# Reading each 4 MB load of keys or values as one contiguous stretch of HBM instead of pieces 256 KB apart

## The chip, the cores and the metric

The kernel runs on one core of a Trainium2 chip. The caches lie in the chip's main memory (HBM). Sixteen DMA engines of the core copy them, packet by packet, into its working memory (SBUF), which has 128 partitions; a kernel asks for such a copy by an instruction on a queue, here that of SP (SyncE). TensorE (PE) multiplies matrices, VectorE (DVE) and ScalarE (ACT) do the rest. The metric is the device time of one execution in microseconds (us). A run of a program on one core is called fast when it lies within 1.5% of the fastest run of the same kernel.

## The reference, cut to what matters

One token attends to a long cache of keys and values. Beside it runs a small gated feed-forward layer, which matters here only because its weights are loaded too.

```python
B, Sq, D = 1, 1, 448
Hq, Hkv, Sk, Dh = 16, 8, 65536, 256           # bf16
k_cache, v_cache: (B, Hkv, Sk, Dh)            # 256 MB (of 2^20 bytes) each
...
scores = einsum("bhqd,bhkd->bhqk", q, k) * Dh ** -0.5
p = softmax(scores, axis=-1)
o = einsum("bhqk,bhkd->bhqd", p, v)
return x + (o reshaped @ wo) + feed_forward(xn)
```

The order in which the 65536 positions of a head are visited is free, so long as keys and values are visited in the same order: the softmax and the weighted sum run over all of them.

## The kernel before: the parts that matter

The ring has four slots of 4 MB (32 KB for each of 128 partitions). Every load fills one slot with 64 rows of 512 B for each partition. The loads go out in one stream from the SP queue, and a load waits only until PE (TensorE) has finished with the slot's former content.

```python
P, CH, NSLOT = 128, 64, 4            # partitions, rows of a partition in a load, slots
FIRST, LAST = [16, 16, 32], [32, 16, 8, 8]     # first and last load are split by rows

def slot_item(key, src, h, n0, parts=None):
    r = rounds[0]; rounds[0] += 1
    s = r % NSLOT
    o = 0
    parts = parts or [("slot%d" % s, CH)]
    for k, (sem, J) in enumerate(parts):
        ap = ring[:, s * SLOT + o * Dh:s * SLOT + (o + J) * Dh]
        item(key + (k,), ap, [(lambda a, J=J: a.rearrange("p (j d) -> p j d", d=Dh),
                               src[0, h].rearrange("(p n) d -> p n d", p=P)[:, n0 + o:n0 + o + J, :])], sem,
             [("FREE", "slot", r - NSLOT)] if r >= NSLOT else None)
        ...

def k_slot(u, c, parts=None):        # half-head u, chunk c; v_slot is the same for values
    slot_item(("k", u, c), A_k_cache, u // 2, (u % 2) * SBN + c * CH, parts)

def prog_sp():                       # the stream of loads
    for key in stream:
        for w in items[key]["need"] or []:
            wait("sp", "pe", w)
        for d, src in items[key]["src"]:
            nc.sync.dma_start(d(items[key]["ap"]), src).then_inc(sems[items[key]["sem"]], 16)
```

With `"(p n) d -> p n d"` and p = 128, partition p owns rows 512p to 512p+511 of a head. A load takes 64 of them: one contiguous piece of 32 KB, and the next partition's piece starts 256 KB further on. PE then transposes the keys (line 382), multiplies them with the query (line 416), and later multiplies the weights of the softmax with the values (line 541).

Of the kernel before, what the change touches and what calls it, by code (L numbers as in the profile page):

```python
# [13 lines left out]
CH = 64  # L14
# [8 lines left out]
def bass_parallel_sum__gqa_block_cached__moe_arch_mod__decode_kernel(  # L23
# [13 lines left out]
    P = 128  # L37
# [223 lines left out]
    def item(key, ap, src, sem, need=None):  # L261
        semtot[sem] = semtot.get(sem, 0) + 16 * len(src)
        items[key] = dict(ap=ap, src=src, sem=sem, val=semtot[sem], need=need)
        stream.append(key)
# [4 lines left out]
    def slot_item(key, src, h, n0, parts=None):  # L269
        r = rounds[0]  # L270
        rounds[0] += 1
# [3 lines that stand above are left out]
        for k, (sem, J) in enumerate(parts):  # L275
            ap = ring[:, s * SLOT + o * Dh:s * SLOT + (o + J) * Dh]
            item(key + (k,), ap, [(lambda a, J=J: a.rearrange("p (j d) -> p j d", d=Dh),
                                   src[0, h].rearrange("(p n) d -> p n d", p=P)[:, n0 + o:n0 + o + J, :])], sem,
                 [("FREE", "slot", r - NSLOT)] if r >= NSLOT else None)
            items[key + (k,)]["rows"] = (n0 + o, J)  # L280
            o += J
        items[key] = dict(parts=len(parts), slot=r)

    def k_slot(u, c, parts=None):
        slot_item(("k", u, c), A_k_cache, u // 2, (u % 2) * SBN + c * CH, parts)

    def v_slot(t, c, parts=None):
        slot_item(("v", t, c), A_v_cache, t // 2, (t % 2) * SBN + c * CH, parts)
# [636 lines left out]
```

## Time and profile before

| | before |
|---|---|
| time | 1291.68 us (1291.57 to 1291.70, 3 runs) |
| bytes loaded | 549 MB (of 10^6 bytes), 22067 packets |
| mean rate | 426 GB/s over the span, 431 GB/s in the middle |
| busy | load queue 99.1% of 16 engines, PE 72%, DVE 43%, ACT 35% |

The page of the kernel before follows: the span, then busy tenths (9 is 90% or more) and GB/s in 40 equal slices, the packets, the queue that carries the loads, and the chain of work that ended last.

```profile
span 1291.1 us, 21412 instructions
...
DMA  9999999999999999999999999999999999999995
GB/s 404 425 433 424 431 432 430 432 429 431 435 428 434 428 434 432 428 435 426 435 433 429 435 427 432 431 432 435 424 436 429 434 431 427 436 429 434 429 431 243
DMA packets 22067, 549.40 MB, mean 426 GB/s; under 512 B 2323, under 2 KB 4374, under 8 KB 4886
...
q1 hardware_dynamic: 22034, 549.04, 99.1%
...
DMA 76%; PE 22%; DVE 1%; ACT 0%; issue 0%; SPq 0%; ACTq 0%
```

The DMA row has no hole before the last slice: loads are queued at all times, or very nearly. The chain contains PE work all the same (22%). A piece of it, in order of time (start, length, what), shows why that is no sign of a PE bound ("issue" is time in which an engine waited for nothing that the profile shows):

```profile
250.73 35.23 DMA ring<-in_A_k_cache_dram
...
293.68 1.90 PE ps_t L382 x16
295.57 0.03 PE ps_s L449 x2
295.60 30.41 DMA ring<-in_A_v_cache_dram
326.01 0.14 issue
326.15 3.29 PE ps_o L541 x32
329.44 0.01 issue
329.46 35.43 DMA ring<-in_A_k_cache_dram
```

Each load in the chain takes 30 to 35 us from its issue to its landing, while 4.19 MB at 431 GB/s need only 9.7 us. So a load stands in a queue of about three loads. The PE pieces of the chain pass while the engines are busy with the loads ahead.

The windows view adds up busy time in stretches. Its columns are the stretch, its length, the busy time of PE, PE's weight loads, DVE, ACT and POOL with instruction counts, the granted clock (the share of TensorE's full clock that its throttle let through), the DMA share and GB/s:

```profile
0.00:30.00 30.00, 15.09 (x216) 13.33 (x216) 15.19 (x33) 9.37 (x16) 4.48 (x34) 1.00 0.96 400
...
300.00:1200.00 900.00, 644.18 (x6678) 465.45 (x6678) 383.34 (x651) 307.80 (x433) 0.00 (x0) 0.85 1.00 431
```

The last two columns say that for 900 us the engines are wholly busy at 431 GB/s.

A busy engine may still be a waiting one: a packet that HBM serves slowly counts as busy (a run further down shows a DMA share of 0.97 at only 383 GB/s). What tells the two apart is how long packets take. The trace has a record of each packet; summed up by size for the kernel before they give (ns):

```
size B   packets  fastest  median    mean   99th pct.
  1792      2048       74      74    76.3       86
  4096       256      159     160   162.3      172
  6272       256      239     239   239.9      251
  8192       404      309     309   312.9      398
 16384       271      611     611   641.7     1099
 32768     16128     1213    1216  1218.1     1227
```

The fastest ones lie on a line. From 4096 to 32768 B it is (1213 - 159) / 28672 = 0.0368 ns for a byte, or 27.2 GB/s for an engine, and 159 - 4096 x 0.0368 = 8.4 ns for a packet. Sixteen engines at 27.2 GB/s make 435 GB/s. The Trainium skill ("DMA: Bandwidth & Descriptors", section "Where 436 GB/s comes from") puts the ceiling of the 16 ports at the same 435 GB/s, and this trace agrees: 431 GB/s in the middle, 1% under it.

### The profile page before, as it was taken

To read this page: it belongs to the slowest core of one execution; us is meant where nothing else is said; L and a number is where in the kernel's file an instruction comes from. 1 tells how busy PE (TensorE), PEld (TensorE's weight loads), DVE (VectorE), ACT (ScalarE), POOL (GpSimd) and SP (SyncE) were. 2 spreads that over 40 slices of the span, in tenths; PEclk is the share of its full clock that TensorE was granted. 3 is DMA by queue.
4 is the path that set the end of the run, shared out by engine and by line. 5 is a ranking of instruction groups with operands and counts; after the bars stand their busy time and mean duration, and the time that the engine had idled before them with its cause. 6 is when DMAs were issued, how large, how long until landed. Compare 5 with 4: busy or idle time off the path is not lost.

```text
span 1291.1 us, 21412 instructions
## 1 busy us (share of the span) xinstructions
PE 934.6 (72%) x9673; PEld 669.9 (52%) x9673; DVE 551.6 (43%) x944; ACT 446.5 (35%) x634; POOL 4.5 (0%) x34
## 2 busy tenths in 40 slices
PE   4988867696666957668587675876669676696665
PEld 4876645464554735546365453654446454474421
DVE  4666435263443625336254352643436353262300
ACT  2556323253332623225233242432424333242300
POOL 1000000000000000000000000000000000000000
PEclk9899879798887988889788897987979888798665
DMA  9999999999999999999999999999999999999995
GB/s 404 425 433 424 431 432 430 432 429 431 435 428 434 428 434 432 428 435 426 435 433 429 435 427 432 431 432 435 424 436 429 434 431 427 436 429 434 429 431 243
DMA packets 22067, 549.40 MB, mean 426 GB/s; under 512 B 2323, under 2 KB 4374, under 8 KB 4886
## 3 DMA queue, kind: packets, MB, share of 16 engines
q1 hardware_dynamic: 22034, 549.04, 99.1%
q8 instruction: 15, 0.25, 0.1%
q14 instruction: 14, 0.11, 0.0%
q10 hardware_dynamic: 4, 0.00, 0.0%
HBM read 549.03 MB, written 0.00 MB: 425 GB/s over the span
## 4 chain that ended last, share of the span: by engine, by line
DMA 76%; PE 22%; DVE 1%; ACT 0%; issue 0%; SPq 0%; ACTq 0%
DMA ring<-in_A_k_cache_dram 42%; DMA ring<-in_A_v_cache_dram 31%; PE ps_t L382 13%; PE ps_o L541 4%; PE ps_q L416 3%; DMA w_area<-in_B_w_down_dram 3%; DMA wr_row<-in_B_w_r_dram 0%; PE ps_s L449 0%; PE ps_t L656 0%; PE ps_m L624 0%; DVE kt_buf L370 0%; ACT S_sb L494 0%; SPq L328 0%; PE ps_m L593 0%; ACT L494 0%
## 5 line engine op out<-in xcount | busy, mean ns | idle before, releaser
L382 PE MATMUL ps_t<-ident_f,ring 128*128 128x128 f32 x4096 | 578.0, 299 | 218.5 <-DMA ring<-in_A_k_cache_dram 217.1
L370 DVE COPY kt_buf<-ps_t 128x1024 bf16<-128x1024 bf16 x768 | 491.9, 685 | 475.8 <-PE ps_t L382 473.6
L382 PEld LDWEIGHTS ps_t<-ident_f,ring 128*128 128x128 f32 x4096 | 502.9, 154 | 343.6 <-DMA ring<-in_A_k_cache_dram 238.5
L372 ACT ACTIVATE kt_buf<-ps_t 128x1024 bf16<-128x1024 bf16 x256 | 261.8, 1023 | 353.3 <-PE ps_t L382 352.9
L394 ACT ACTIVATE s<-ps_q 98x512 bf16<-98x512 f32 x256 | 152.7, 596 | 319.6 <-PE ps_q L416 319.6
L541 PE MATMUL ps_o<-ring,p_sb 128*4 128x512 bf16 x2048 | 158.4, 462 | 108.6 <-DMA ring<-in_A_v_cache_dram 98.4
L416 PE MATMUL ps_q<-kt_buf,q_cur 128*2 128x512 bf16 x2048 | 169.0, 407 | 0.7 <-ACT s L394 0.7
L541 PEld LDWEIGHTS ps_o<-ring,p_sb 128*4 128x4 bf16 x2048 | 52.2, 95 | 203.1 <-issue 144.9
L557 DVE CAST ob_sb<-ps_o 100x512 bf16<-100x512 f32 x15 | 10.4, 692 | 184.4 <-PE ps_o L541 184.4
L449 PEld LDWEIGHTS ps_s<-sel_bf,s 128*128 128x128 bf16 x1024 | 64.5, 99 | 11.4 <-issue 6.9
L449 PE MATMUL ps_s<-sel_bf,s 128*128 128x8 bf16 x1024 | 64.0, 168 | 0.5 <-ACT s L394 0.5
L485 ACT ACTIVATE p_sb<-S_sb 128x128 bf16<-128x128 bf16 x64 | 17.1, 303 | 101.7 <-PE ps_o L541 101.5
L416 PEld LDWEIGHTS ps_q<-kt_buf,q_cur 128*2 128x2 bf16 x2048 | 26.2, 79 | 6.9 <-ACT s L394 1.2
L514 DVE RECIPROCAL rs<-ps_m 128x4 f32<-128x4 f32 x15 | 2.7, 182 | 45.8 <-PE ps_m L521 45.8
L593 PE MATMUL ps_m<-wo_cur,oT_sb 128*1 128x448 bf16 x56 | 15.4, 406 | 0.0
L494 ACT ACTIVATE S_sb<-S_sb,negmax 128x512 bf16<-128x512 bf16 x16 | 13.3, 860 | 5.1 <-DVE negmax L477 5.1
L521 PEld LDWEIGHTS ps_m<-rowsum,ones_f 128*128 128x128 f32 x60 | 8.6, 207 | 7.4 <-issue 7.4
L429 DVE CAST S_sb<-ps_s 128x512 bf16<-128x512 f32 x16 | 10.9, 681 | 1.9 <-PE ps_s L449 1.9
L431 DVE TENSOR_REDUCE m1p<-S_sb 128x2 f32<-128x512 bf16 x16 | 11.0, 686 | 0.6
L469 PE MATMUL ps_m<-ident_f,m 128*2 128x128 f32 x15 | 4.2, 277 | 9.0 <-DVE m L437 9.0
L585 DVE TENSOR_TENSOR rowsf<-ps_m,rowsf 1x448 f32<-1x448 f32 x14 | 8.6, 612 | 4.6 <-PE ps_m L593 4.3
L521 PE MATMUL ps_m<-rowsum,ones_f 128*128 128x2 f32 x60 | 9.9, 270 | 0.0
(68 smaller groups left out, 91.6 us busy)
## 6 DMA issues: line engine op xcount, KB each, us to landing
ring<-in_A_k_cache_dram SPq DMA_DIRECT2D x63, 4096.0 KB, 33.6
ring<-in_A_v_cache_dram SPq DMA_DIRECT2D x63, 4096.0 KB, 30.4
w_area<-in_A_wq_dram SPq DMA_DIRECT2D x1, 3584.0 KB, 11.4
wo_cur<-in_A_wo_dram SPq DMA_DIRECT2D x7, 448.0 KB, 25.6
ring<-in_A_k_cache_dram SPq DMA_DIRECT2D x2, 1024.0 KB, 14.5
ring<-in_A_k_cache_dram SPq DMA_DIRECT2D x1, 2048.0 KB, 20.9
ring<-in_A_v_cache_dram SPq DMA_DIRECT2D x1, 2048.0 KB, 30.3
w_area<-in_B_w_gate_dram SPq DMA_DIRECT2D x1, 1568.0 KB, 39.0
```

The source lines that it names most:

```text
L370: op(e, ("EV", s, m), lambda x: x.tensor_copy(out=kt[:, :], in_=tb[:, :]), f"ev{m}")
L372: op(e, ("EV", s, m), lambda x: x.activation(out=kt[:, :], in_=tb[:, :], func=ACTF.Copy), f"ev{m}")
L382: ins = nc.tensor.matmul(ps_tf[m][:, jj * P:(jj + 1) * P], lhsT=kv[:, j + GN * m + jj, :], rhs=ident_f[:, :], is_transpose=True, start=Tru ...
L394: op("act", ("EVQ", s), lambda e: e.activation(out=s2[s % 2][0:QROWS, :], in_=ps_q[0:QROWS, :], func=ACTF.Copy), "evq")
L416: ins = nc.tensor.matmul(ps_q[32 * m:32 * m + rep, 0:512], lhsT=q_cur[:, hf, :], rhs=kt[:, :].rearrange("p (k f) -> p f k", f=NH)[:, hf, : ...
L431: op("dve", ("SMAX", b), lambda e: e.tensor_reduce(out=m1p[:, :, k], in_=S.rearrange("p n i -> p i n"), axis=AX.X, op=ALU.max))
L449: ins = nc.tensor.matmul(o, lhsT=s2[s % 2][:, jj * P:(jj + 1) * P], rhs=sel_bf[:, :, :], start=True, stop=True)
L485: op("act", ("PC", t, c), lambda e: e.activation(out=p_sb[:, c, :, :], in_=S_sb[t // 2 % 2][:, n:n + CH, :], func=ACTF.Copy), "pc")
L494: op("act", ("EXPI", h, i), lambda e, i=i: e.activation(out=S[:, :, i], in_=S[:, :, i], func=ACTF.Exp, bias=negmax[:, i:i + 1], scale=1.0, ...
L521: ins = nc.tensor.matmul(ps_m[0:P, C_TOT + f * rep:C_TOT + (f + 1) * rep], lhsT=ones_f[:, :], rhs=rowsum[:, :], start=True, stop=True)
L541: ins = nc.tensor.matmul(ps_o[32 * g:32 * g + 2 * rep, :], lhsT=p_sb[:, c, o + j:o + j + 2, :].rearrange("p n i -> p (n i)"), rhs=kv[:, j: ...
L593: ins = nc.tensor.matmul(dst, lhsT=oT_sb[:, hf, i:i + 1], rhs=wo[:, i, hf, :], start=(hf == 0 and i == 0), stop=(hf == NH - 1 and i == rep ...
```

## The change

The intent is to give HBM an easier task: a load reads one stretch of 4 MB, partition p taking rows 64p to 64p+63 of it, in place of 128 pieces spread over the 32 MB of a head. The whole diff is one line:

```diff
-                                   src[0, h].rearrange("(p n) d -> p n d", p=P)[:, n0 + o:n0 + o + J, :])], sem,
+                                   src[0, h].rearrange("(c p j) d -> c p j d", p=P, j=CH)[n0 // CH, :, o:o + J, :])], sem,
```

Keys and values go through the same line, so both are permuted alike and the result stays right. No instruction, wait or semaphore changes.

## The prediction

> **What bounds the kernel now.** The DMA engines do. The page's DMA row is 9 in 39 of 40 slices of the 1291.1 us span; the queue that loads everything is busy 99.1% of 16 engines' span and moves 549.04 MB at a mean of 426 GB/s. The windows view shows a DMA share of 1.00 and 430 to 432 GB/s in stretches from 140 to 1040 us. PE is busy 72%, DVE 43%, ACT 35%. The chain of waits is 76% DMA (42% key loads, 31% value loads) and its PE pieces (13% key transposes) end where a slot comes free for the next load, while other loads are still queued: the DMA row has no hole there. The Trainium skill ("DMA: Bandwidth & Descriptors", Where 436 GB/s comes from) puts the ceiling of the 16 ports at 435 GB/s; this trace's 432 is 1% under it.
>
> **What the change does.** Before, partition p reads 64 rows of 512 B, 32 KB in one piece, and the next partition's piece lies 256 KB further; after, it lies 32 KB further and the whole load is one 4 MB stretch. So bytes (549 MB), loads (126 of 4 MB and the split ones) and packets (22067, of them 16128 of 32 KB by the trace's DMA records) should not change. Keys and values are permuted alike, so no compute instruction, wait or semaphore changes.
>
> **What is to be won.** By the trace's DMA records the 32 KB packets are very uniform: fastest 1213 ns, median 1216, mean 1218, 95th percentile 1224; 32768 B in 1216 ns on 16 engines is 431 GB/s. HBM locality can only shorten what is over the fastest: 5 ns times 1008 packets for each engine, 5.1 us or 0.4% of the span. Of this only some 0.4 to 0.7 us is true stalls (25 packets of 1592 to 1875 ns); the rest looks like the engine's own rhythm and should stay. The trace holds contiguous loads already: w_q, w_gate, w_up. The packets of gate and up (12544 B) take 469 to 474 ns, or 26.6 GB/s for an engine, the later w_q packets (28672 B) about 1062 ns, 27.0 GB/s; the strided 32 KB ones make 26.9. So contiguous reads run at the same pace.
>
> **What could be lost.** The same section's page (Latency and other measured facts, HBM row pitch) tells of lower rates at pitches of 512 KB and more. This trace shows none of it at 256 KB. The contiguous weight loads show no loss from engines reading side by side. For 2% slower the mean 32 KB packet would have to grow by about 26 ns (25.8 us over 1008 packets), to 1244.
>
> **Prediction.** The loads lie on the critical path, but the engines set their pace, not HBM. I predict 1291.2 us, 8 in 10 between 1287 and 1295. Chances: faster by over 2% 0.01, within 2% 0.96, slower by over 2% 0.03.
>
> **What would show it.** Right: 22067 packets again, 16128 of 32 KB at a median near 1216 ns, 430 to 432 GB/s in the middle stretches, 99% busy queue. Wrong, faster: packets under 1213 ns, or a mean rate above 432. Wrong, slower: the DMA row still at 9 but longer packets and fewer GB/s; or more packets, if the flat source were cut in other pieces.
>
> **What would make it wrong.** Merging of the flat source into other descriptors (fewer engines or other packet sizes), or HBM conflicts among 16 engines within one 4 MB stretch. The weight loads speak against both, but are short.

## The result, and the profile after

| | time, us | ratio to before, fast runs | 95% interval |
|---|---|---|---|
| after | 1292.29 median (1291.75 to 1292.85, 4 runs) | 1.0002 | 0.9987 to 1.0016 |
| after, again with 5 rounds | 1292.39 median (1291.66 to 1292.76, 5 runs) | 1.0001 | 0.9987 to 1.0014 |

A ratio is the mean time of one kernel's fast runs over the mean of the other's of the same rounds, so it is not quite the ratio of the medians. In the first comparison before had 1291.69 us (1291.57 to 1293.01, 4 runs), in the second 1291.92 us (1291.75 to 1292.93, 9 runs). The runs of both kernels are spread over the same 1291.6 to 1293.0 us, so a difference of half a microsecond between the medians says nothing.

The same lines of the page of the changed kernel:

```profile
span 1291.1 us, 21412 instructions
...
DMA  9999999999999999999999999999999999999995
GB/s 401 428 432 422 434 432 428 434 429 432 432 431 431 428 431 432 432 433 428 432 432 431 432 429 431 431 432 432 429 434 428 434 428 431 436 428 432 430 432 244
DMA packets 22068, 549.42 MB, mean 426 GB/s; under 512 B 2323, under 2 KB 4374, under 8 KB 4886
...
q1 hardware_dynamic: 22034, 549.04, 99.1%
...
DMA 77%; PE 21%; issue 0%; ACT 0%; DVE 0%; SPq 0%; DVEq 0%
```

and of its windows view:

```profile
0.00:30.00 30.00, 15.07 (x216) 13.26 (x216) 15.19 (x33) 9.41 (x16) 4.52 (x34) 1.00 0.97 400
...
300.00:1200.00 900.00, 645.15 (x6677) 463.70 (x6677) 383.42 (x651) 307.80 (x433) 0.00 (x0) 0.84 1.00 431
```

The load queue carries 22034 packets in both kernels (the one packet more in the total is an instruction fetch), at the same rate in the same stretches. The 32 KB packets, 16128 again, take 1213 ns at the fastest, 1218 in the median and 1218.1 in the mean; before had 1213, 1216 and 1218.1. Nothing was won and nothing was given back: the change did not touch what sets the pace.

### The profile page after: what moved, and what is told of

It reads as the page before. It is cut to its first block, busy times and chain, and to the rows that moved or that the text cites. A ratio compares the mean times of both kernels' runs of the same rounds, so it can differ in the third digit from the quotient of the medians.

```text
span 1291.1 us, 21412 instructions
## 1 busy us (share of the span) xinstructions
PE 932.1 (72%) x9673; PEld 666.8 (52%) x9673; DVE 551.7 (43%) x944; ACT 446.6 (35%) x634; POOL 4.5 (0%) x34
## 3 DMA queue, kind: packets, MB, share of 16 engines
q1 hardware_dynamic: 22034, 549.04, 99.1%
## 4 chain that ended last, share of the span: by engine, by line
DMA 77%; PE 21%; issue 0%; ACT 0%; DVE 0%; SPq 0%; DVEq 0%
DMA ring<-in_A_k_cache_dram 43%; DMA ring<-in_A_v_cache_dram 31%; PE ps_t L382 13%; PE ps_o L541 4%; PE ps_q L416 3%; DMA w_area<-in_B_w_down_dram 3%; PE ps_s L449 0%; PE ps_t L656 0%; SPq L328 0%; DVE kt_buf L370 0%; ACT S_sb L494 0%; PE ps_m L593 0%; ACT L494 0%; ACT kt_buf L372 0%; PE ps_m L521 0%
## 5 line engine op out<-in xcount | busy, mean ns | idle before, releaser
L593 PE MATMUL ps_m<-wo_cur,oT_sb 128*1 128x448 bf16 x56 | 19.6, 492 | 0.0
```

The source lines that it names most:

```text
L593: ins = nc.tensor.matmul(dst, lhsT=oT_sb[:, hf, i:i + 1], rhs=wo[:, i, hf, :], start=(hf == 0 and i == 0), stop=(hf == NH - 1 and i == rep ...
```

## The experiments

Theory A says that the loads bound the kernel and that the engines' own pace sets the loads: about 8.4 ns for each packet and 27.2 GB/s for each engine. Where a piece lies in HBM then does not matter; only how long it is. Rival B says that locality in HBM sets a part of the pace, and that 256 KB between pieces merely happens to be harmless, or that a gain is hidden. Rival C says that the slots come free too late, so that compute sets the time and the DMA row only looks full.

Twelve kernels ran, one of them the changed kernel again, as told above. Its expectation was:

> The changed kernel once more, unaltered, with more rounds, to narrow the interval of the result. Theory A: ratio to before within 0.997 to 1.003, 1290 to 1294 us. Rival B (a real small gain or loss of locality): an interval that leaves 1 out.

A warning for all that follows: every one of these kernels passed the comparison with the reference, those with wrong rows included. Which rows were read it evidently cannot tell; an average over 65536 random rows is small beside x, which would explain it. That the change is right rests on keys and values sharing one line of code, not on that comparison.

### Half of the bytes: is it the loads?

```diff
+            L = J if r < NSLOT else J // 2
-             ... (lambda a, J=J: a.rearrange("p (j d) -> p j d", d=Dh), ... [:, n0 + o:n0 + o + J, :])
+             ... (lambda a, L=L: a[:, :L * Dh].rearrange("p (j d) -> p j d", d=Dh), ... [:, n0 + o:n0 + o + L, :])
```

> The kernel before, but every load of keys or values after the first four slots fetches only the first 32 of its 64 rows for each partition (16 KB pieces, same pitch of 256 KB); the compute works on what the slot holds, so all instructions but the loads' size stay and the result is wrong on purpose. Theory A (the DMA engines' pace bounds the whole kernel): bytes fall from 549 to about 290 MB, 16 KB packets take about 611 ns each, the loads alone would need about 680 us, so the time falls by over 15% to what the compute needs, estimated 950 to 1100 us from PE's 935 us busy. Rival C (the slots come free too late, i.e. compute sets the time and the DMA row only looks full): within 2% of 1292 us.

Measured: 872.64 us, ratio 0.6752 (0.6733 to 0.6772). From its page (busy share, DMA row, chain):

```profile
PE 820.1 (94%) x9673; PEld 602.5 (69%) x9673; DVE 544.0 (63%) x944; ACT 446.4 (51%) x634; POOL 4.5 (1%) x34
...
DMA  9998668789697888979877896978789697778966
...
PE 85%; DVE 6%; DMA 5%; ACT 2%; issue 1%; SPq 0%
```

With the same compute instructions, the chain is now 85% PE, and the DMA row has the holes that it lacks in both kernels. Rival C falls: the compute alone fits in 873 us, a third less than the kernel takes. My estimate of what the compute needs (950 to 1100 us, from PE's 935 us busy) was too high. PE was busy only 820 us here, with a transpose at 277 ns in place of 299 and a mean granted clock of 0.984 in place of 0.848. The Trainium skill ("TensorE: Matmul & The Clock Gate", section "Part 1: The HAM clock gate (the "warmup" mystery)") says that the clock is halved after an idle window of about 3.4 us and restored after a busy one of that length. The trace of before agrees: after a wait of 4.99 us for a value load, the 32 value matmuls ran in 3.47 us at a granted clock of 0.57; shortly before, at a clock of 1.00, 32 of them took 1.90 us. So PE's busy time in a kernel that waits for loads is no measure of what PE needs when it need not wait.

### Half of the bytes, contiguous

The same kernel, whose loads after the first four slots read one stretch of 2 MB each:

```diff
-  src[0, h].rearrange("(p n) d -> p n d", p=P)[:, n0 + o:n0 + o + L, :]
+  (... "(c p j) d -> c p j d", p=P, j=CH)[n0 // CH, :, o:o + L, :] if r < NSLOT else
+   ... "(c p j) d -> c p j d", p=P, j=CH // 2)[n0 // CH, :, o // 2:o // 2 + L, :])
```

> The kernel with half of the bytes (872.6 us), whose loads after the first four slots each read one contiguous 2 MB stretch instead of 16 KB pieces 256 KB apart (wrong result on purpose). Here the loads' queue was busy 82% and PE 94%, so the loads have slack. Theory A: the same as its strided twin within 1%, and the same 609 to 611 ns for the median 16 KB packet. Rival B: the mean 16 KB packet, which was 646 ns in the twin because of slow ones after each pause, falls clearly; the time would still hardly move.

Measured: 871.90 us, ratio 0.6746 (0.6726 to 0.6766), the same as its strided twin. The 16 KB packets took 611 ns in the median of both, and 652 against 646 ns in the mean. So in a kernel whose loads have pauses the contiguous form did not shorten the slow packets after a pause either.

The pauses settle one rival more that was not named beforehand: 431 GB/s could be a limit that all 16 engines share, as a ceiling of HBM for this core would be. In the strided run 98 of the 16 KB packets ran while on average fewer than 6 load packets were open (counted from the DMA records). A shared limit would have let them go faster; their median was 611 ns, the same as with all engines at work. So the pace is one that each engine has for itself. Whether the engine sets it, its way into SBUF or its own way to HBM, no run varies.

### The best locality there is

Every load of the changed kernel reads the same first 4 MB of head 0:

```diff
-  src[0, h].rearrange("(c p j) d -> c p j d", p=P, j=CH)[n0 // CH, :, o:o + J, :]
+  src[0, 0].rearrange("(c p j) d -> c p j d", p=P, j=CH)[0, :, o:o + J, :]
```

> The changed kernel, but every load reads the same first 4 MB of head 0 of its tensor (wrong result on purpose): the best locality in HBM that can be had. Theory A (engine pace of about 8.5 ns for each packet plus 27.2 GB/s): no gain, 1290 to 1294 us, 32 KB packets still at 1213 to 1218 ns. Rival B (HBM locality sets part of the pace): faster than 1286 us, packets under 1213 ns.

Measured: 1292.88 us, ratio 1.0004 (0.9975 to 1.0033). The 32 KB packets: 1213 ns fastest, 1218 median, 1218.1 mean. The few long ones over 1300 ns are 25 here, 25 before and 26 after, so these are no matter of locality either. The middle of the run, from its windows view:

```profile
300.00:1200.00 900.00, 645.54 (x6677) 464.08 (x6677) 383.45 (x651) 307.86 (x433) 0.00 (x0) 0.84 1.00 431
```

There was nothing to be won from locality.

### Partitions 512 KB and 2 MB apart

Now the other way: the pieces stay at 32 KB, and partition p reads from rows further away, in other heads (wrong, every byte still read once). G is 8 for 2 MB and 2 for 512 KB:

```diff
-  src[0, h].rearrange("(p n) d -> p n d", p=P)[:, n0 + o:n0 + o + J, :]
+  src[0, h // G * G:h // G * G + G].rearrange("g s d -> (g s) d").rearrange("(p n) d -> p n d", p=P)[
+      :, h % G * NPP + n0 + o:h % G * NPP + n0 + o + J, :]
```

> The kernel before with the partitions' pieces 2 MB apart instead of 256 KB: partition p reads its p-th 2 MB of the whole cache, a 32 KB piece for each load, every byte once (wrong result on purpose). Theory A in its strong form (the place in HBM never matters at 32 KB pieces): 1290 to 1294 us. Rival B (distance in HBM matters, 256 KB is merely still harmless): the Trainium skill's row pitch entry suggests a loss of about a quarter at 2 MB for copies within HBM, which would give over 1500 us; any packets over 1250 ns in the mean speak for it.

> Partitions 512 KB apart, 32 KB pieces (wrong result on purpose), between before's 256 KB and the 2 MB that cost 0.45%. Theory A2: 1291 to 1295 us, at most a small loss at the start. Rival B (cost grows with the distance): a share of the 5.7 us, over 1294 us.

The row pitch entry is that of "DMA: Bandwidth & Descriptors", section "Latency and other measured facts"; the 1500 us are an estimate from it.

Measured: 1298.18 us at 2 MB, ratio 1.0045 (1.0016 to 1.0074); 1292.22 us at 512 KB, ratio 1.0001 (0.9982 to 1.0019). So 512 KB costs nothing and 2 MB a little. The windows view of the 2 MB run shows where:

```profile
0.00:30.00 30.00, 14.72 (x189) 13.36 (x190) 13.59 (x30) 7.24 (x14) 4.51 (x34) 0.94 0.89 348
...
300.00:1200.00 900.00, 641.55 (x6709) 462.56 (x6709) 383.53 (x652) 308.93 (x435) 0.00 (x0) 0.86 1.00 431
```

The first 30 us ran at 348 GB/s in place of 400: (400 - 348) x 30 us = 1.6 MB, or 3.6 us at 431 GB/s. After that the rate is near that of before (431 GB/s from 300 to 1200 us). In those 30 us the 8 KB packets took up to 388 ns on average in a stretch of 1.5 us, against 309 before. So the strong form of theory A is wrong, and rival B has a true core: the place in HBM can cost time. But it does so only for a while at the start and, as shown below, in the last loads, and only at a distance well beyond that of either kernel.

Do the short pieces at the start (the first load is split in 8, 8 and 16 KB) make that loss? A run with the first load whole:

```diff
-FIRST = [16, 16, 32]
+FIRST = [64]
```

> The run with partitions 2 MB apart, with the first 4 MB of keys as one load of 32 KB pieces and not split in 8, 8 and 16 KB pieces (wrong result on purpose). That run lost its 5.7 us in the first 30 us, where 8 KB packets took up to 388 instead of 309 ns and 1.4 MB fewer had come by 25 us. Theory A2 (pieces far apart in HBM cost only while the 16 engines still start in step, in short pieces): 32 KB packets slow only at the start, well under 1.4 MB lost by 25 us, 430 GB/s afterwards. Rival B (a lasting cost of the 2 MB distance): a mean rate under 428 GB/s from 100 to 1200 us.

Measured: 1297.29 us, ratio 1.004 (1.0022 to 1.0058).

```profile
0.00:30.00 30.00, 10.23 (x161) 9.45 (x162) 11.00 (x27) 5.62 (x12) 4.48 (x34) 1.00 0.97 383
30.00:60.00 30.00, 30.00 (x336) 24.41 (x335) 22.27 (x36) 19.11 (x24) 0.00 (x0) 1.00 0.98 402
60.00:100.00 40.00, 33.06 (x349) 26.79 (x342) 24.77 (x40) 19.59 (x25) 0.00 (x0) 0.91 1.02 431
...
300.00:1200.00 900.00, 645.20 (x6709) 464.80 (x6701) 383.19 (x651) 308.01 (x434) 0.00 (x0) 0.85 1.00 431
```

By 25 us from the first packet this run was 0.5 MB behind the kernel before (10.0 against 10.5 MB), as theory A2 had it. But the loss only came later (383 and then 402 GB/s in the first two stretches) and was of the same size in the end: at 100 us from the first packet the load queue had moved 41.3 MB against 42.7 before. The splitting only moves it. The loss passes in both runs: the middle runs at 431 GB/s. That it ends when the 16 engines have drifted apart is a guess that no run tests.

It comes back at the end. By the DMA records, counted from each run's first load packet, the first 25 MB landed 3.7 us later than in the kernel before (2.7 us in the run with the first load whole), the first 545 MB 4.1 us later (2.9), but the last of the 549 MB 5.7 us later (5.3). In the last 20 us of the loads, where the last load is split too, 8 KB packets took 364 ns in the mean (392) against 314 before, and 4 KB packets 194 ns (202) against 162. So a part of the 0.45% is lost there, which theory A2 did not foresee. Why is open.

### Shorter pieces, in one stretch and scattered

These runs separate the two things that "contiguous" can mean: that the whole load is one stretch, and that each partition's piece is long. In the first the load is one stretch of 4 MB, dealt out in pieces of 8 rows (4 KB). In the second the same 4 KB pieces lie scattered over the head's 32 MB. In the third they lie over the whole cache, partitions 2 MB apart (wrong).

```diff
+  # one stretch:   "(c a p r) d -> c p a r d", p=P, a=CH // 8, r=8)[n0 // CH, :, o // 8:(o + J) // 8]
+  # over 32 MB:    "(p a c r) d -> c p a r d", p=P, a=CH // 8, r=8)[n0 // CH, :, o // 8:(o + J) // 8]
+  # over 256 MB:   "(p a c r) d -> c p a r d" on all heads' rows, [h * 2 * HC + n0 // CH, :, ...]
```

> Each 4 MB load reads one contiguous stretch, dealt out to the partitions in pieces of 8 rows (4 KB): partition p takes 8 pieces that lie 512 KB apart. Correct order for keys and values. Theory A (8.5 ns for each packet + 27.2 GB/s): 8 packets of 159 to 160 ns for 1218 ns before, 58 us more in all, about 1350 us (1335 to 1365). Rival B (one contiguous stretch is what counts): within 1% of 1292 us.

> The same 4 KB pieces and the same packets as the run with 4 KB pieces of one stretch, but a load's pieces are scattered over the 32 MB of a head: partitions 256 KB apart, a partition's 8 pieces 32 KB apart. Theory A: the same time as its contiguous twin within 1%. Rival B (locality in HBM counts, 32 KB pieces only hid it): slower than the twin by over 2%.

> 4 KB pieces, partitions 2 MB apart and a partition's 8 pieces 256 KB apart (wrong result on purpose), against 1359 us for 4 KB pieces in one stretch or scattered over 32 MB. Theory A (packet pace alone): 1355 to 1370 us, the start's loss included. Rival B (far pieces cost when they are short): over 1385 us, with 4 KB packets well over 164 ns or gaps in the middle of the run.

Measured: 1359.21 us in one stretch, ratio 1.0516 (1.0486 to 1.0547); 1359.17 us over 32 MB, ratio 1.0516 (1.0486 to 1.0547); 1360.02 us over 256 MB, ratio 1.0525 (1.0506 to 1.0545). The windows view of each, in this order:

```profile
300.00:1200.00 900.00, 624.42 (x6409) 451.65 (x6408) 369.37 (x625) 298.19 (x422) 0.00 (x0) 0.83 1.03 409
```

```profile
300.00:1200.00 900.00, 623.74 (x6415) 454.71 (x6414) 369.94 (x627) 298.95 (x423) 0.00 (x0) 0.84 1.03 409
```

```profile
300.00:1200.00 900.00, 624.67 (x6413) 452.57 (x6414) 369.33 (x626) 298.46 (x423) 0.00 (x0) 0.84 1.03 409
```

All three run at 409 GB/s. At that rate an engine spends 16 x 4096 / 409 = 160 ns on a packet, where the fastest 4 KB packets of the kernel before, one of the two points of the fitted line, took 159. (The records themselves say 164 ns in the mean; the DMA share of 1.03 tells that successive packets overlap a little in them.) One stretch is worth nothing at 4 KB either, while shorter pieces cost 5%. This is the clearest case for theory A: with the packets held equal, three layouts in HBM give one time; with the stretch kept whole and the packets cut, the time grows by what the packets cost.

### Pieces of one row, 512 B

Two runs at the far end: rows dealt out in turn from one 4 MB stretch, and single rows scattered over 32 MB.

```diff
+  # one stretch:  "(c j p) d -> c p j d", p=P, j=CH)[n0 // CH, :, o:o + J, :]
+  # scattered:    "(p j c) d -> c p j d", p=P, j=CH)[n0 // CH, :, o:o + J, :]
```

> Each 4 MB load reads one contiguous stretch of HBM as in the change, but rows are dealt out in turn: partition p takes rows p, p+128, ... so each piece of a partition is one row of 512 B, 8192 pieces for a load. Correct result, same order for keys and values. Theory A (cost is by packet: 8.5 ns + bytes/27.2 GB/s, fitted from before's packet sizes): 64 packets of about 27 ns, 1750 ns for what one 32 KB packet did in 1218, so about 1830 us (1750 to 1950). Rival B (what counts is that a load is one contiguous stretch of HBM): within 2% of 1292 us.

> The 512 B pieces of the run at 1896 us, but scattered over the 32 MB of a head: partitions 256 KB apart, a partition's 64 pieces 4 KB apart, where the twin read one contiguous 4 MB. Theory A: about 1896 us again, within 2%. Rival B (locality counts at small pieces): slower by over 2%. Less sure than for 4 KB: every 512 B piece is a place of its own in HBM here, and the twin's packets already took 119 ns, which is longer than the 84 ns that a single 2 KB piece takes.

Measured: 1896.02 us in one stretch, ratio 1.4671 (1.4629 to 1.4714), far from rival B's 1292 us; 2200.21 us scattered, ratio 1.7023 (1.6974 to 1.7073). The second misses what theory A expected of it (1896 us within 2%), but the pair is not a fair one. The pages count the packets:

```profile
DMA packets 268724, 549.41 MB, mean 290 GB/s; under 512 B 2323, under 2 KB 6422, under 8 KB 268310
```

```profile
DMA packets 1053620, 549.42 MB, mean 250 GB/s; under 512 B 2323, under 2 KB 1052950, under 8 KB 1053206
```

In the one stretch, four neighbouring partitions' rows are neighbours in HBM as well, and the records hold 261632 packets of 2 KB; scattered, there are 1048576 of 512 B. So it is luck that the first time came near the 1830 us of theory A, which counted packets of 512 B. For a packet of 2 KB the fitted line gives 84 ns, and 16 of them for one of 32 KB make about 1420 us in all (an estimate); the records show 118.8 ns in the mean. Theory A's sum misses both runs at 512 B, by some 480 and 370 us: something else costs time there. Besides, issuing a load is no longer cheap. The timeline of the SP queue (start, length, what) shows the two runs at 512 B, one stretch first:

```profile
365.39 13.98 SPq L328 DMA_DIRECT2D ring<-in_A_v_cache_dram  x1
```

```profile
308.68 17.16 SPq L328 DMA_DIRECT2D ring<-in_A_k_cache_dram  x1
```

An issue took 0.33 us in the kernel before. Here it takes 14 to 17 us, and in the timeline of the one-stretch run the issues start 14.4 us apart when back to back, which for 4.19 MB is 291 GB/s, the measured rate. This time is not the instruction's own work. In the one-stretch run a load of wo, of only 256 packets, took 14.3 to 15.5 us to issue (seven times) where it stood behind such a load, and the load of 8192 pieces behind it took 0.70 us. So an issue waits for what is ahead of it. Whether that is the engines, or the making of the packets for the load ahead, is not told apart, nor is locality from packet count. At 512 B the question of locality stays open.

## Why the prediction was right

- **The bound.** Predicted: the engines, by a full DMA row, a 99.1% busy queue and 431 GB/s under a ceiling of 435. Shown: with half of the bytes the same compute took 873 us, so the loads are what the 1292 us are spent on. And 16 KB packets that ran while most engines paused took the same 611 ns, so the pace is each engine's own.
- **What changes.** Predicted: bytes, packets and waits stay. Measured: 22034 packets on the load queue, 16128 of 32 KB, in both.
- **What is to be won.** Predicted: at most the 5.1 us by which the 32 KB packets exceed their fastest, and in truth little of it, as most looked like the engine's own rhythm. Measured: none of it. Even with every load reading the same 4 MB the mean stayed at 1218.1 ns, so this excess does not come from where the data lies. (The 25 long packets exceed the fastest by 0.8 us for each engine, a little more than the 0.4 to 0.7 us of the prediction.)
- **The precedent.** The prediction read the pace of contiguous loads from the weight loads in the trace of before (12544 B packets in 469 to 474 ns). That was its strongest evidence, and it held.
- **What could be lost.** The prediction named the HBM row pitch entry of the Trainium skill and found no trace of it at 256 KB. The runs bound this: none at 512 KB, 0.45% at 2 MB, lost at the start and at the end.
- **The size.** 1291.2 us predicted, 1292.29 measured, inside the range of 1287 to 1295. The granted clock and the busy times of PE, DVE and ACT stayed as they were.

No experiment points to a version that beats both kernels by a layout of the caches: the pieces are 32 KB already, and by the fitted line all that longer ones could save is a part of 8.4 in 1213 ns.

## What to carry to other kernels

Before making a large load contiguous as a whole, see how long each partition's piece is and how long its packets take: here packets that took their fastest time were shortened by no layout of the source. (Other destinations were not tried.) Pieces of 32 KB ran at 431 GB/s wherever they lay, pieces of 4 KB at 409 whether in one stretch or scattered; between these two the length of the piece is what to buy. And to learn whether a full DMA row is the true bound, halve the bytes and see how far the time falls.

## What the Trainium skill lacked or had wrong

- "DMA: Bandwidth & Descriptors", section "Latency and other measured facts", entry on HBM row pitch: for copies between HBM tensors in rows of 16 KiB it gives 207 GB/s at a pitch of 512 KiB and 164 at 2 MiB. For loads from HBM to SBUF in pieces of 32 KB, these runs show no loss at 512 KB (1292.22 us, 431 GB/s) and at 2 MB a loss in the first 60 us and in the last loads (1298.18 us; 348 GB/s in the first 30 us, 431 in the middle). The entry does not say that the loss can pass.
- The same page, section "Where 436 GB/s comes from": its note that for transfers between HBM and SBUF the HBM side (about 358 GB/s) binds did not hold here: 431 GB/s for a program on one core. "HBM Reference", section "Specifications (TRN2)", says as much (about 425 GB/s for a core alone), so the note should say when it holds.
- The same page gives a rate for loads issued from SP on trn2 at one length of piece alone (408.7 GB/s for 4 KiB rows, in a table about iDMA), which these runs confirm with 409. They add 431 GB/s at 32 KB and 250 to 290 at 512 B; the fastest packets fit 8.4 ns + bytes / 27.2 GB/s from 4 KB to 32 KB.
- The same page, section "Anatomy of one DMA", calls descriptor generation small, for the GpSimd path. No page says how long the SP queue is held up behind a load of many pieces: an issue took 0.33 us behind loads of 128 pieces of 32 KB, 14 to 17 us behind loads of 8192 pieces of 512 B.
- "TensorE: Matmul & The Clock Gate" was right and explains a miss of mine. Nothing was lacking; these runs add a size for a kernel bound by loads: PE's busy time was 935 us at a granted clock of 0.848, and 820 us at 0.984 for the same instructions once the loads no longer held it up.
